# An attention and gMLP stack on one core: SyncE's queue in program order, later row sums, moved residual loads, a third buffer

## The chip, the cores and the metric

The kernel runs on one core of a Trainium2 chip. The metric is the device time of one execution in microseconds (us), the lower the better. Engines are written as in the profile: PE is the TensorE matmul, DVE the VectorE, ACT the ScalarE, POOL the GpSimd, and SP the SyncE, which here only issues DMA transfers.

## The reference, cut to what matters

```python
# x: 1 x 2048 x 512, bf16
def _A_ref(x, mem0, Wq, Wk, Wv, Wo, seg_len=32):     # attention with a memory of 8 rows
    mem = mem0
    for s in range(64):                              # one segment after the other
        h = concat([mem, x[:, 32*s:32*s+32]])        # 40 rows
        q, k, v = h @ Wq, h @ Wk, h @ Wv             # 32 heads of 128
        o = softmax(mask(q @ k.T * scale)) @ v       # per head
        o = o @ Wo
        mem = o[:, :8]                               # goes into the next segment
        outs.append(o[:, 8:])

def _B_ref(x, w_in, w_sp, b_sp, w_out):              # gMLP
    z = gelu(x @ w_in)                               # 2048 x 1376
    z1, z2 = z[..., :688], layernorm(z[..., 688:])
    g = w_sp @ z2 + b_sp[:, None]                    # over all 2048 rows
    return (z1 * g) @ w_out

for _ in range(2):                                   # same weights both times
    x = x + _A_ref(layernorm(x), ...)
    x = x + _B_ref(layernorm(x), ...)
```

The 64 segments of one attention block form a chain through `mem`. A gMLP has a stage of projections (16 row tiles of 128 rows, `x @ w_in`) and a stage of gates (16 tiles, `w_sp @ z2`, then `w_out`).

## The kernel before

PE, DVE and ACT keep the order in which the program was written (`ORDERED`). POOL and SP are ordered by the scheduler of the kernel's framework when the program is built. An engine's queue runs in its order.

```python
ORDERED = {PE, DVE, Activation}                                  # names shortened

# _consts: at the start
    nc.scalar.dma_start(bsp_bf[:], b_sp.rearrange("(t p) -> p t", p=P))
    nc.gpsimd.tensor_copy(bsp[:], bsp_bf[:])                     # POOL also issues the weight loads

# class _Rows: rows between attention and gMLP
    def apply(self, tb, MV, RS, first=False, x=None):            # normalise a row tile for attention
        # ... DVE writes xn
        nc.sync.dma_start(self.xn_d[...], xn[:])                 # store, then eight loads that wait for it
        # ... 4 x nc.sync.dma_start(preB[...], self.xn_d[...])
        # ... 4 x nc.sync.dma_start(pre, self.xn_d[...])

    def y_load(self, tb, first, eng, x=None, o=None):            # residual x and attention output o
        # ... eng.dma_start(x, ...), 4 x eng.dma_start(o <- oA_d), 4 x eng.dma_start(o <- oB_d)

    def y_add(self, tb, first, eng):
        o, x = self.y[tb]
        eng.tensor_tensor(out=..., in0=o, in1=x, op=ALU.add)     # the residual sum
        self.nc.sync.dma_start(self.xd[tb * P:(tb + 1) * P, :], o)

# b_block: the gMLP
        wsp_pool = ctx.enter_context(tc.tile_pool(name="b_wsp", bufs=2))
        ctx.enter_context(tc.manual_schedule(engines=ORDERED))

        def load_xnT(tt):                                        # transposed load, 3 buffers
            nc.sync.dma_start_transpose(out=xnT[tt][:], in_=rows.xb_d[...])
        def late_load(tb):                                       # the last four row tiles are summed here
            rows.y_load(tb, first, nc.gpsimd, x=..., o=o[:])
            rows.y_add(tb, first, nc.gpsimd)
        # late_norm(tb): DVE statistics and normalisation of two late tiles, SP stores them to xb_d

        for tt in range(3):
            load_xnT(tt)
        # ... w_out on POOL
        for tb in (NT - 4, NT - 3):
            late_load(tb)
        for tt in range(NT):
            project(tt)                                          # 12 matmuls into pz, two Gelu on ACT, DVE statistics
            if tt + 3 < NT:
                load_xnT(tt + 3)
            if tt in (3, 6):
                late_norm(NT - 4 + 2 * (tt // 6))
            if tt == 3:
                for tb in (NT - 2, NT - 1):
                    late_load(tb)
            if tt in (8, 11):
                load_wsp(tt // 11)
            if tt % 2 == 1:
                # ... DVE: RSz and NBz of two tiles
            elif tt > 1:
                normalise(tt - 2)                                # ACT: z2n
                normalise(tt - 1)
        # gates: gate(t), with product(t) behind it, which calls load_wsp(t + 2);
        # finish(t) writes rows t, and for t < 2 calls rows.apply(t, ...)

# a_block: after each segment s (tb, j4 = s // 4, s % 4)
            def spare():
                # ... if j4 == 3: rows.apply(tb + 2, ...)
            def tail():
                # ...
                if due:
                    ys.append(due.pop(0))
                    rows.y_load(ys[0], first, nc.sync)           # summed in the next segment
```

The softmax here doesn't subtract the row's maximum and nothing guards it: scores larger than these inputs give would overflow.

Of the kernel before, what the change touches and what calls it, by code (L numbers as in the profile page):

```python
# [14 lines left out]
P = 128  # L15
DM = 512
# [34 lines left out]
def _consts(ctx, tc, c, b_sp):  # L51
# [43 lines left out]
    c["maskM"] = maskM  # L95
    bsp_bf = tmp.tile([P, 16], BF16, name="bsp_bf")
    nc.scalar.dma_start(bsp_bf[:], b_sp.rearrange("(t p) -> p t", p=P))
    nc.gpsimd.tensor_copy(bsp[:], bsp_bf[:])
    c["bsp"] = bsp
    tctx.close()  # L100
    c.update(ident_bf=ident_bf, maskN=maskN, ones=ones, onesG=onesG)
# [37 lines left out]
class _Rows:  # L139
# [5 lines left out]

    def load(self, tb, first, eng):

        t = self.pool.tile([P, DM], BF16 if first else F32, name="ln_xb" if first else "ln_x")
        eng.dma_start(t[:], (self.x_in if first else self.xd)[tb * P:(tb + 1) * P, :])
        self.xs[tb] = t  # L150

    def apply(self, tb, MV, RS, first=False, x=None):
        nc = self.nc
        x = self.xs.pop(tb)[:] if x is None else x
        xn = self.pool.tile([P, DM], BF16, name="ln_xn", bufs=2)
        nc.vector.tensor_scalar(out=_perm(xn[:]) if first else xn[:], in0=_nat(x) if first else x, scalar1=MV[:, tb, 0:1],
                                scalar2=RS[:, tb:tb + 1], op0=ALU.subtract, op1=ALU.mult)
        nc.sync.dma_start(self.xn_d[M + tb * P:M + (tb + 1) * P, :], xn[:])
        preB = self.pool.tile([P, P], BF16, name="preB", bufs=2)
        for cg in range(4):  # L160
            nc.sync.dma_start(preB[32 * cg:32 * cg + 32, :],
                              self.xn_d[M + tb * P:M + (tb + 1) * P, 128 * cg:128 * cg + 128]
                              .rearrange("(j r) c -> j r c", j=4)[:, 24:32, :])
        self.preB[tb] = preB
        for j4 in range(4):
            t0 = tb * P + 32 * j4
            t = self.pool.tile([P, P], BF16, name="pre", bufs=9)
            nc.sync.dma_start(t[:], self.xn_d[t0:t0 + 32, :].rearrange("r (cg c) -> cg r c", cg=4))
            self.pre[4 * tb + j4] = t

    def y_load(self, tb, first, eng, x=None, o=None):
        if x is None:
            x = self.pool.tile([P, DM], BF16 if first else F32, name="y_xb" if first else "y_x")[:]
            o = self.pool.tile([P, DM], F32, name="y_o")[:]
        eng.dma_start(x, (self.x_in if first else self.xd)[tb * P:(tb + 1) * P, :])
        ot = o.rearrange("p (cg c) -> p cg c", cg=4)
        for j in range(4):
            eng.dma_start(ot[32 * j:32 * j + 24], self.oA_d[4 * tb + j + 1].rearrange("(cg r) c -> r cg c", cg=4)[8:32])
            r0 = 32 * (tb % 4) + 8 * j
            eng.dma_start(ot[32 * j + 24:32 * j + 32], self.oB_d[tb // 4, r0:r0 + 8, :].rearrange("r (cg c) -> r cg c", cg=4))  # L180
        self.y[tb] = (o, x)
# [18 lines left out]
def b_block(tc, c, rows, xd, MV_in, RS_in, MV_out, RS_out, w_in, w_sp, w_out, S, first, out_final=None):  # L200
# [4 lines left out]
    with ExitStack() as ctx:  # L205
        wp = ctx.enter_context(tc.tile_pool(name="b_w", bufs=1))
        mid = ctx.enter_context(tc.tile_pool(name="b_mid", bufs=1))
        gp = ctx.enter_context(tc.tile_pool(name="b_g", bufs=2))
        wsp_pool = ctx.enter_context(tc.tile_pool(name="b_wsp", bufs=2))
        zp = ctx.enter_context(tc.tile_pool(name="b_z", bufs=2))  # L210
        ps_pool = ctx.enter_context(tc.tile_pool(name="b_ps", bufs=1, space=PSUM))
        big = _Tagged(ps_pool, "big", 2)
        one = _Tagged(ps_pool, "one", 2)
        ctx.enter_context(tc.manual_schedule(engines=ORDERED))


        w_in_sb = wp.tile([P, KT, FF], BF16, name="w_in_sb")
# [17 lines left out]
            nc.sync.dma_start_transpose(out=xnT[tt][:], in_=rows.xb_d[tt * P:(tt + 1) * P, :].rearrange("t (kt s) -> t kt s", s=P))  # L235

        def late_load(tb):
            x = gp.tile([P, DM], F32, name="xs")[:]
            o = gp.tile([P, DM], F32, name="xo")
            rows.y_load(tb, first, nc.gpsimd, x=x[:, 0:DM // 2].bitcast(BF16) if first else x, o=o[:])  # L240
            rows.y_add(tb, first, nc.gpsimd)

        def late_norm(tb):
# [33 lines left out]
        for tt in range(NT):  # L277
            project(tt)
            if tt + 3 < NT:
                load_xnT(tt + 3)  # L280
            if tt in (3, 6):
                late_norm(NT - 4 + 2 * (tt // 6))
            if tt == 3:
                for tb in (NT - 2, NT - 1):
                    late_load(tb)
            if tt in (8, 11):
                load_wsp(tt // 11)
            if tt % 2 == 1:
                _rstd_dve(nc, zp, RSz[:, tt - 1:tt + 1], MVz[:, tt - 1:tt + 1, 1], 2)
                nc.vector.scalar_tensor_tensor(out=NBz[:, tt - 1:tt + 1], in0=MVz[:, tt - 1:tt + 1, 0], scalar=-1.0,  # L290
                                               in1=RSz[:, tt - 1:tt + 1], op0=ALU.mult, op1=ALU.mult)
            elif tt > 1:
                normalise(tt - 2)
                normalise(tt - 1)
# [15 lines left out]

        def product(t):
            del wsp[t]
            if t + 2 < NT:
                load_wsp(t + 2)
            u[t] = gp.tile([P, FH], BF16, name="u", bufs=1)
            nc.vector.scalar_tensor_tensor(out=u[t][:].rearrange("p (k f) -> p k f", k=2), in0=pg.pop(t)[:, 0:2, 0:344],
                                           scalar=c["bsp"][:, t:t + 1], in1=z1[:, t, :].rearrange("p (k f) -> p k f", k=2),
                                           op0=ALU.add, op1=ALU.mult)
            load_x(t)

        def turn_u(t):
# [1 line left out]
            for fc, (f0, fsz) in enumerate(FCH):  # L323
                nc.tensor.transpose(pT[0:fsz, fc * P:(fc + 1) * P], u[t][:, f0:f0 + fsz], ident_bf[:])
            del u[t]
            uT[t] = gp.tile([P, 6, P], BF16, name="uT")
            nc.scalar.copy(uT[t][:, 0:5, :].rearrange("p fc r -> p (fc r)"), pT[:, 0:640])
            nc.scalar.copy(uT[t][0:48, 5, :], pT[0:48, 640:768])

        def finish(t):  # L330
# [3 lines left out]
            del uT[t]  # L334
            xs = xt.pop(t)
            if out_final is not None:
                xob = gp.tile([P, DM], F32, name="xo")[:, 0:DM // 2].bitcast(BF16)
                nc.vector.tensor_tensor(out=_nat(xob), in0=_nat(py[:]), in1=_perm(xs[:]), op=ALU.add)
                nc.scalar.dma_start(out_final[t * P:(t + 1) * P, :], xob)
                return  # L340
            xo = gp.tile([P, DM], F32, name="xo")
            nc.vector.tensor_tensor(out=_perm(xo[:]), in0=_nat(py[:]), in1=_perm(xs[:]), op=ALU.add)
            nc.scalar.dma_start(xd[t * P:(t + 1) * P, :], xo[:])
            _stats(nc, zp, xo[:], MV_out[:, t, :])
# [18 lines left out]
def kernel(  # L363
# [34 lines left out]
    with tc.manual_schedule(engines=ORDERED):  # L398
        _ln_exp_table(nc)
        for tt in range(2):  # L400
            x = rp.tile([P, DM], BF16, name="x0", tag=("ln_xb", "y_xb")[tt])
            nc.sync.dma_start(x[:], x_in[tt * P:(tt + 1) * P, :])
            rows.xs[tt] = x
        m0 = rp.tile([M, DM], BF16, name="m0", tag="ln_xn", bufs=2)
        nc.sync.dma_start(m0[:], A_mem0.rearrange("b m d -> (b m) d"))
# [5 lines left out]
        _ln_consts(ctx, tc, c)  # L411
        MV, RS = c["MV"], c["RS"]
        for tt in range(2):
            _stats(nc, rp, rows.xs[tt][:], MV[0][:, tt, :])
            _rstd_act(nc, RS[0][:, tt:tt + 1], MV[0][:, tt, 1:2], c)
            rows.apply(tt, MV[0], RS[0], first=True)
        _consts(ctx, tc, c, B_b_sp)
# [30 lines left out]
def a_block(tc, c, rows, MV_in, RS_in, MV_out, RS_out, wqkv, Wo, S, first):  # L448
# [6 lines left out]
    with ExitStack() as ctx:  # L455
# [304 lines left out]
        for s in range(NSEG):  # L760
# [8 lines left out]
            def spare():  # L769
# [2 lines left out]
                if j4 == 0 and tb + 1 < NB:  # L772
                    ln_turn(tb + 1)
                if j4 == 2 and tb + 2 < NB and first:
                    _stats(nc, rows.pool, rows.xs[tb + 2][:], MV_in[:, tb + 2, :])
                    copies.append(lambda: _rstd_act(nc, RS_in[:, tb + 2:tb + 3], MV_in[:, tb + 2, 1:2], c))
                if j4 == 3 and tb + 2 < NB:
                    rows.apply(tb + 2, MV_in, RS_in, first=first)
# [1 line left out]
            def tail():  # L780
                if ys:
                    rows.y_norm(ys.pop(0), MV_out, RS_out)
                if tb % 4 == 3 and j4 == 0 and tb > 4:
                    due.extend(range(tb - 7, tb - 3))
                if due:
                    ys.append(due.pop(0))
                    rows.y_load(ys[0], first, nc.sync)

# [49 lines left out]
```

## Time and profile before

| | before |
|---|---|
| time, three first runs | 1990.4 to 1996.4 us, median 1995.61 |
| span of the profiled run, mean granted PE clock (1 is full speed) | 1993.9 us, 0.979 |
| PE, DVE, ACT, POOL busy | 90%, 63%, 53%, 7% |

A ledger of stages was made from marks in the timelines: the first and last masked copy (CAST_PREDICATED) that DVE makes in each attention block, the first `pz` matmul of PE and the last `NBz` of DVE in each gMLP. In us:

| stage | before |
|---|---|
| start, to the first masked copy | 62.0 |
| attention 1 | 743.1 |
| to the first `pz` | 27.7 |
| projections 1, to the last `NBz` | 69.5 |
| gates 1, to the first masked copy of attention 2 | 141.1 |
| attention 2 | 741.0 |
| to the first `pz` | 26.5 |
| projections 2 | 69.4 |
| gates 2, to the end | 113.7 |

Two groups of the page's costliest groups tell where PE waits. The columns are line, engine, operation, output and inputs, shapes and count; then busy time and mean ns; then the idle time ahead of the group and what ended most of it. Kernel before:

```profile
L489 PE MATMUL psm<-Wq_sb,hA 128*32 128x512 bf16 x4096 | 278.9, 388 | 28.7 <-DVE hA L598 27.7
L258 PE MATMUL pz<-w_in_sb,xnT 128*128 128x512 bf16 (+1 forms) x384 | 91.4, 405 | 44.6 <-ACT z L262 27.6
```

The first is the start of a segment in attention: 28.7 us of waits in 128 segments, nearly all for DVE's `hA`. The second is the projections of both gMLPs: 44.6 us of waits, mostly for ACT.

### The profile page before, as it was taken

The page shows a single profiled execution, that of the slowest core. Times are in us where ns is not written, and L with a number is a line of the kernel's source. Part 1 is how long each engine was busy: PE and PEld are TensorE (multiplying, and loading weights), DVE is VectorE, ACT ScalarE, POOL GpSimd, SP SyncE. Part 2 cuts the span into 40 slices and gives each one's busy share as a digit, 9 for nine tenths or more (in the row PEclk, how much of TensorE's full clock was granted, in tenths as well). Part 3 has the DMA queues.
Part 4 walks back from the last instruction along what each step waited for, and adds up shares of the span by engine and source line. Part 5 has one row for each costly group of instructions (what it writes and reads, how often), then busy time and mean ns, then how long its engine had stood idle before and what let it go on. Part 6 is the DMA issues. An engine that isn't in the chain of part 4 may idle for free.

```text
span 1993.9 us, 94918 instructions
## 1 busy us (share of the span) xinstructions
PE 1797.8 (90%) x43776; PEld 1035.5 (52%) x43776; DVE 1259.0 (63%) x2875; ACT 1047.9 (53%) x1880; POOL 138.0 (7%) x288
## 2 busy tenths in 40 slices
PE   2999999989998999777989999999899989996798
PEld 0555555545554555334545555555455555553355
DVE  1677677777777667572346667767767767774522
ACT  1566666656665666452136566666566656663411
POOL 5000000000000000230010000000000000005000
PEclk9999999999999999989999999999999999998899
DMA  8200000020012000625650000001200110017254
GB/s 306 69 21 20 18 19 17 24 79 17 18 30 73 18 15 29 152 72 123 148 155 24 20 20 22 21 20 50 69 21 21 60 58 22 15 53 187 55 139 111
DMA packets 179935, 120.08 MB, mean 60 GB/s; under 512 B 117280, under 2 KB 156976, under 8 KB 179536
## 3 DMA queue, kind: packets, MB, share of 16 engines
q1 hardware_dynamic: 158864, 70.43, 13.9%
q0 software_dynamic: 9376, 28.88, 4.4%
q10 hardware_dynamic: 11296, 14.70, 2.4%
q8 instruction: 342, 5.60, 1.2%
q14 instruction: 57, 0.47, 0.1%
HBM read 59.29 MB, written 33.69 MB: 47 GB/s over the span
## 4 chain that ended last, share of the span: by engine, by line
PE 37%; DVE 7%; ACT 5%; DMA 3%; issue 2%; SPq 1%; POOL 1%; POOLq 0%; DVEq 0%; ACTq 0%
PE psm L489 12%; PE pg L308 6%; PE pw L546 5%; PE psb L489 4%; DVE KA L626 2%; PE py L333 2%; ACT rows L622 2%; ACT E L650 2%; PE psO L669 2%; PE psS L646 1%; PE pwB L555 1%; DMA wspT<-in_B_w_sp_dram 1%; DVE E L653 1%; PE psM L713 1%; PE psD L722 1%
## 5 line engine op out<-in xcount | busy, mean ns | idle before, releaser
L489 PEld LDWEIGHTS <-hA 128*32 128x32 bf16 x12288 | 311.3, 97 | 329.1 <-DVE hA L598 64.3
L622 ACT CAST rows<-psm 128x512 bf16<-128x512 f32 x512 | 299.8, 586 | 197.9 <-PE psm L489 197.9
L489 PE MATMUL psm<-Wq_sb,hA 128*32 128x512 bf16 x4096 | 278.9, 388 | 28.7 <-DVE hA L598 27.7
L546 PE MATMUL pw<-Wo_sb,uT 128*32 128x128 bf16 x16640 | 267.4, 220 | 28.8 <-issue 20.2
L546 PEld LDWEIGHTS <-uT 128*32 128x32 bf16 x16640 | 245.2, 97 | 69.5 <-issue 30.8
L489 PE MATMUL psm<-Wk_sb,hA 128*32 128x512 bf16 x4096 | 273.7, 385 | 0.0
L489 PE MATMUL psv<-Wv_sb,hA 128*32 128x512 bf16 x4096 | 268.0, 382 | 0.0
L626 DVE STREAM_TRANSPOSE QQ<-rows 128x512 bf16<-128x512 bf16 x256 | 182.0, 711 | 95.6 <-ACT rows L622 94.5
L685 DVE TENSOR_TENSOR uT<-psO,Rt 128x384 bf16<-128x384 f32 x256 | 138.1, 539 | 126.5 <-ACT Rt L675 126.5
L626 DVE STREAM_TRANSPOSE KA<-rows 128x512 bf16<-128x512 bf16 x256 | 182.0, 711 | 42.8 <-ACT rows L622 41.0
L650 ACT ACTIVATE E<-psS 128x448 bf16<-128x448 f32 x256 | 140.0, 547 | 107.6 <-PE psS L646 107.6
L308 PE MATMUL pg<-z2n,wspT 128*128 128x344 bf16 x1024 | 166.1, 316 | 14.9 <-ACT z2n L269 7.6
L632 DVE CAST VA<-psv 128x512 bf16<-128x512 f32 x256 | 175.7, 686 | 2.3
L591 POOL COPY QQ<-QTB 128x256 bf16<-128x256 bf16 x128 | 51.2, 401 | 1431.3 <-PE psS L646 870.1
L646 PEld LDWEIGHTS <-KA 128*64 128x64 bf16 x2048 | 79.8, 113 | 127.8 <-DVE KA L626 126.5
L675 ACT ACTIVATE Rt<-Rt 128x1024 f32<-128x1024 f32 x128 | 135.4, 1058 | 4.1
L308 PEld LDWEIGHTS <-wspT 128*128 128x128 bf16 x1024 | 96.5, 99 | 71.5 <-issue 15.5
L258 PE MATMUL pz<-w_in_sb,xnT 128*128 128x512 bf16 (+1 forms) x384 | 91.4, 405 | 44.6 <-ACT z L262 27.6
L489 PEld LDWEIGHTS <-hB 128*32 128x32 bf16 x3072 | 75.9, 97 | 106.4 <-issue 38.4
L674 ACT ACTIVATE Rt<-psD 128x1024 f32<-128x1024 f32 x128 | 128.6, 1005 | 0.0
L730 DVE TENSOR_TENSOR uT<-psO,Rm 128x128 bf16<-128x128 f32 x256 | 62.8, 286 | 93.3 <-PE psO L669 93.1
L646 PE MATMUL psS<-QQ,KA 128*64 128x80 bf16 x2048 | 109.9, 208 | 10.1
(113 smaller groups left out, 2265.1 us busy)
## 6 DMA issues: line engine op xcount, KB each, us to landing
oA_d<-o_sb SPq DMA_DIRECT2D x130, 64.0 KB
Wo_sb<-in_A_Wo_dram POOLq DMA_DIRECT2D x8, 1024.0 KB, 13.5
xs<-xd ACTq DMA_DIRECT2D x32, 256.0 KB
xd<-y_o SPq DMA_DIRECT2D x24, 256.0 KB
y_o<-oA_d SPq DMA_DIRECT2D x96, 48.0 KB
Wq_sb<-in_A_Wq_dram POOLq DMA_DIRECT2D x8, 512.0 KB, 7.4
Wk_sb<-in_A_Wk_dram POOLq DMA_DIRECT2D x8, 512.0 KB, 11.1
xn_d<-ln_xn SPq DMA_DIRECT2D x32, 128.0 KB
```

The source lines that it names most:

```text
L258: nc.tensor.matmul(pz[:, c0:c1], lhsT=xnT[tt][:, kt, :], rhs=w_in_sb[:, kt, c0:c1], start=(kt == 0), stop=(kt == KT - 1))
L308: nc.tensor.matmul(pg[t][:, k, 0:344], lhsT=wsp[t][:, st, :], rhs=z2n[:, st, 344 * k:344 * k + 344], start=(st == 0), stop=(st == NT - 1))
L489: nc.tensor.matmul(ps[32 * cg:32 * cg + 32, :], lhsT=lhs(kt, cg), rhs=rhs(kt, cg), start=(kt == 0), stop=(kt == KT - 1), tile_position=(0, ...
L546: nc.tensor.matmul(po[32 * cg:32 * cg + 32, 0:128], lhsT=lhs[:, n, :], rhs=wo_rhs(h, cg), start=(h == 0), stop=(h == H - 1), tile_position ...
L622: nc.scalar.copy(r[:], ps[:])
L626: nc.vector.transpose(out=QQ[:, j % 2, :, 0:32] if j < 2 else KA[:, j % 2], in_=r[:])
L632: nc.vector.tensor_copy(VA[:, r].rearrange("p i e -> p (i e)"), ps)
L646: nc.tensor.matmul(pS[64 * g:64 * g + 64, i, c0:80 if K is KA else 112], lhsT=K[:, r, n:n + 2, :].rearrange("p h k -> p (h k)"), rhs=q if ...
L650: nc.scalar.activation(out=E[:, r], in_=pS, func=ACT.Exp, scale=scale)
L674: nc.scalar.activation(out=o, in_=in_, func=ACT.Ln)
L675: nc.scalar.activation(out=o, in_=o, func=ACT.Exp, scale=-1.0)
L685: nc.vector.tensor_tensor(out=hview(uT_nxt, 2 * r, 2 * r + 2, 8, 32), in0=oview(2 * r, 2 * r + 2, 8, 32), in1=Rr[:, :, :, 0:24], op=ALU.mult)
```

## The change

The diff has four intents. The cast of `bsp` leaves POOL, whose queue the first weights stand in. A residual load of a segment is no longer written where the next block's rows are (j4 = 3). The `wspT` tiles of the gates get a third buffer. In the gMLP SP joins the engines in program order, and the last four row tiles are normalised later (after tiles 5 and 9 instead of 3 and 6). To make room in memory, some row tiles share buffers.

```diff
-    nc.gpsimd.tensor_copy(bsp[:], bsp_bf[:])
+    nc.vector.tensor_copy(bsp[:], bsp_bf[:])
... (bf16 row tiles become views of float32 tiles: load, y_load)
-        wsp_pool = ctx.enter_context(tc.tile_pool(name="b_wsp", bufs=2))
+        wsp_pool = ctx.enter_context(tc.tile_pool(name="b_wsp", bufs=3))
-        ctx.enter_context(tc.manual_schedule(engines=ORDERED))
+        ctx.enter_context(tc.manual_schedule(engines=ORDERED | {mybir.EngineType.SP}))
         def late_load(tb):
-            x = gp.tile([P, DM], F32, name="xs")[:]
-            o = gp.tile([P, DM], F32, name="xo")
-            rows.y_load(tb, first, nc.gpsimd, x=x[:, 0:DM // 2].bitcast(BF16) if first else x, o=o[:])
+            x, o = None, None
+            if tb % 2:
+                x = gp.tile([P, DM], F32, name="xs")[:]
+                o = gp.tile([P, DM], F32, name="xo", bufs=1)[:]
+            rows.y_load(tb, first, nc.gpsimd, x=x, o=o)
             rows.y_add(tb, first, nc.gpsimd)
-            if tt in (3, 6):
-                late_norm(NT - 4 + 2 * (tt // 6))
-            if tt == 3:
+            if tt in (5, 9):
+                late_norm(NT - 4 + 2 * (tt // 9))
+            if tt == 5:
                 for tb in (NT - 2, NT - 1):
                     late_load(tb)
-            if tt in (8, 11):
-                load_wsp(tt // 11)
+            if tt in (9, 11, 13):
+                load_wsp((tt - 9) // 2)
-            if t + 2 < NT:
-                load_wsp(t + 2)
+            if t + 3 < NT:
+                load_wsp(t + 3)
... (uT and xo with one buffer)
-                if due:
+                if due and (j4 != 3 or tb + 2 >= NB):
```

More of the change, by code (lines that the diff above doesn't have):

```diff
@@ L146, in load @@
     def load(self, tb, first, eng):
-        t = self.pool.tile([P, DM], BF16 if first else F32, name="ln_xb" if first else "ln_x")
-        eng.dma_start(t[:], (self.x_in if first else self.xd)[tb * P:(tb + 1) * P, :])
+        t = self.pool.tile([P, DM], F32, name="ln_x")[:]
+        t = t[:, 0:DM // 2].bitcast(BF16) if first else t
+        eng.dma_start(t, (self.x_in if first else self.xd)[tb * P:(tb + 1) * P, :])
         self.xs[tb] = t
@@ L153, in apply @@
         nc = self.nc
-        x = self.xs.pop(tb)[:] if x is None else x
+        x = self.xs.pop(tb) if x is None else x
         xn = self.pool.tile([P, DM], BF16, name="ln_xn", bufs=2)
@@ L172, in y_load @@
         if x is None:
-            x = self.pool.tile([P, DM], BF16 if first else F32, name="y_xb" if first else "y_x")[:]
+            x = self.pool.tile([P, DM], F32, name="y_x")[:]
             o = self.pool.tile([P, DM], F32, name="y_o")[:]
+        x = x[:, 0:DM // 2].bitcast(BF16) if first else x
         eng.dma_start(x, (self.x_in if first else self.xd)[tb * P:(tb + 1) * P, :])
@@ L325, in turn_u @@
             del u[t]
-            uT[t] = gp.tile([P, 6, P], BF16, name="uT")
+            uT[t] = gp.tile([P, 6, P], BF16, name="uT", bufs=1)
             nc.scalar.copy(uT[t][:, 0:5, :].rearrange("p fc r -> p (fc r)"), pT[:, 0:640])
@@ L336, in finish @@
             if out_final is not None:
-                xob = gp.tile([P, DM], F32, name="xo")[:, 0:DM // 2].bitcast(BF16)
+                xob = gp.tile([P, DM], F32, name="xo", bufs=1)[:, 0:DM // 2].bitcast(BF16)
                 nc.vector.tensor_tensor(out=_nat(xob), in0=_nat(py[:]), in1=_perm(xs[:]), op=ALU.add)
@@ L340, in finish @@
                 return
-            xo = gp.tile([P, DM], F32, name="xo")
+            xo = gp.tile([P, DM], F32, name="xo", bufs=1)
             nc.vector.tensor_tensor(out=_perm(xo[:]), in0=_nat(py[:]), in1=_perm(xs[:]), op=ALU.add)
@@ L400 @@
         for tt in range(2):
-            x = rp.tile([P, DM], BF16, name="x0", tag=("ln_xb", "y_xb")[tt])
-            nc.sync.dma_start(x[:], x_in[tt * P:(tt + 1) * P, :])
+            x = rp.tile([P, DM], F32, name="x0", tag=("ln_x", "y_x")[tt])[:, 0:DM // 2].bitcast(BF16)
+            nc.sync.dma_start(x, x_in[tt * P:(tt + 1) * P, :])
             rows.xs[tt] = x
@@ L413 @@
         for tt in range(2):
-            _stats(nc, rp, rows.xs[tt][:], MV[0][:, tt, :])
+            _stats(nc, rp, rows.xs[tt], MV[0][:, tt, :])
             _rstd_act(nc, RS[0][:, tt:tt + 1], MV[0][:, tt, 1:2], c)
@@ L774, in spare @@
                 if j4 == 2 and tb + 2 < NB and first:
-                    _stats(nc, rows.pool, rows.xs[tb + 2][:], MV_in[:, tb + 2, :])
+                    _stats(nc, rows.pool, rows.xs[tb + 2], MV_in[:, tb + 2, :])
                     copies.append(lambda: _rstd_act(nc, RS_in[:, tb + 2:tb + 3], MV_in[:, tb + 2, 1:2], c))
```

## The prediction

> **What bounds the kernel now.** I read the page first, then each stage by its own timelines and waits.
>
> ```profile
> span 1993.9 us, 94918 instructions
> PE 1797.8 (90%) x43776; PEld 1035.5 (52%) x43776; DVE 1259.0 (63%) x2875; ACT 1047.9 (53%) x1880; POOL 138.0 (7%) x288
> ...
> PE   2999999989998999777989999999899989996798
> ...
> DMA  8200000020012000625650000001200110017254
> ```
>
> PE is the bound, at 90%. A slice of the 40 is 49.8 us. PE is short in the first slice (start), in slices 17 to 19 and 37 to 38 (the two gMLPs, 820 to 1022 us and 1806 to 1994), and by a tenth in a few slices of the attention blocks. Elsewhere PE is full and this change leaves PE's own work alone: in the comparison of the two programs' orders PE's list is the same, 87,554 rows. So only PE's holes can change. There are four kinds, one for each part of the change.
>
> **Start.** The timeline of POOL:
>
> ```profile
> 12.54 0.41 POOL L79 TENSOR_SCALAR_AFFINE_SELECT maskf<-maskf 32x32 f32<-32x32 f32 x2
> 19.63 0.20 POOL L98 CAST bsp<-bsp_bf 128x16 f32<-128x16 bf16 x1 [6.68 <-DMA bsp_bf<-in_B_b_sp_dram]
> 20.09 0.56 POOL L442 DMA_DIRECT2D Wq_sb<-in_A_Wq_dram  x1 [0.27 <-issue]
> ```
>
> POOL sits 6.68 us before a tiny cast, and the other 16 weight loads stand behind it. The windows table has 383 to 390 GB/s from 8 to 16 us, 82 GB/s from 16 to 20, near 400 from 28 on; PE then follows the weights until its first segment at 49.17.
>
> **Attention.** DVE writes one CAST_PREDICATED (L597) per 32-row segment. The distance between two of them is a segment: about 11.8 us, about 12.5 with a residual sum. Four pairs stand out: 15.93 and 14.63 (from 426.7), 15.66 and 13.02 (from 623.1), 15.38 and 13.50 (from 1408.3), 17.34 and 12.94 (from 1601.9). Timelines of SP and DVE in the third:
>
> ```profile
> 1412.41 2.18 SPq L168 DMA_DIRECT2D pre<-xn_d  x4
> 1414.71 0.41 SPq L603 DMA_DIRECT2D oA_d<-o_sb  x1
> 1415.22 0.38 SPq L197 DMA_DIRECT2D xb_d<-ln_xn  x1
> 1415.65 0.40 SPq L178 DMA_DIRECT2D y_o<-oA_d  x1
> ...
> 1421.31 0.69 DVE L185 TENSOR_TENSOR y_o<-y_o,y_x 128x512 f32<-128x512 f32 x1 [3.84 <-DMA y_o<-oB_d]
> ```
>
> The fourth residual load of a group stands on SP behind the next block's rows (`preB`, `pre`). It starts at 1415.65 instead of about 1411.5, DVE waits 3.84 us in order, and hA, then PE, wait behind it. PE's next 64 matmuls take 5.35 us instead of 3.55, at a lower clock.
>
> **gMLP, projections.** PE's timeline, first gMLP:
>
> ```profile
> 832.78 9.77 PE L258 MATMUL pz<-w_in_sb,xnT 128*128 128x512 bf16 x36 [5.58 <-issue]
> 845.76 10.75 PE L258 MATMUL pz<-w_in_sb,xnT 128*128 128x512 bf16 x48 [3.21 <-DMA xnT<-xb_d]
> 862.48 6.26 PE L258 MATMUL pz<-w_in_sb,xnT 128*128 128x512 bf16 x24 [5.97 <-ACT z L262]
> 881.00 11.88 PE L258 MATMUL pz<-w_in_sb,xnT 128*128 128x512 bf16 x48 [6.45 <-ACT z L262]
> ```
>
> PE isn't the limit here. From 884 to 902 NBz comes every 6.15 us for a pair of tiles, a loop through ACT (z, z2n) and DVE (statistics, 13 small operations). The late rows add 5.3 us of DVE work per pair of rows (two such pairs), and the second one waits some 1.5 us for POOL. The 3.21 us is tile 3's transposed load, behind two `wspT` transposes.
>
> **gMLP, gates.** The same timeline later has four holes in the first gMLP:
>
> ```profile
> 928.81 1.92 PE L308 MATMUL pg<-z2n,wspT 128*128 128x344 bf16 x12 [1.09 <-DMA wspT<-in_B_w_sp_dram]
> 940.52 3.60 PE L308 MATMUL pg<-z2n,wspT 128*128 128x344 bf16 x12 [4.80 <-DMA wspT<-in_B_w_sp_dram]
> 956.20 1.92 PE L308 MATMUL pg<-z2n,wspT 128*128 128x344 bf16 x12 [0.39 <-DMA wspT<-in_B_w_sp_dram]
> 977.42 1.92 PE L308 MATMUL pg<-z2n,wspT 128*128 128x344 bf16 x12 [0.88 <-DMA wspT<-in_B_w_sp_dram]
> ```
>
> The second gMLP has none: a gate there takes 6.73 us throughout.
>
> **What the Trainium skill says.** "DMA: Bandwidth & Descriptors", section "Anatomy of one DMA — SWDGE (gpsimd) path": DMA engines do not wait on semaphores; the wait happens on the issuing sequencer before dispatch. The trace agrees: SP's store of the first late sum is issued at 845.44, right after POOL ends it at 845.41, and nothing else passes on SP in between. So a store that waits holds up every load written behind it; my main point rests on this. The same section gives a fixed cost of about 2 us for such a load; here the chain has 2.42 us for `xo<-oB_d`. "TensorE: Matmul & The Clock Gate", Part 1: PE's clock is halved after idleness and comes back after some microseconds of work; the trace agrees (granted clock 0.50 at 832 to 836 and at 880 to 884, after the holes).
>
> **The change part by part.**
>
> 1. *The cast of `bsp` to DVE.* POOL ends its masks at about 13, so the weights start some 7 us earlier. They bound the start until 49.17; small row loads compete with them. **-6 us**. DVE's cast stands after memsets that end at 27.6, when `bsp_bf` has landed: nothing.
> 2. *Residual loads not at j4 = 3.* In the order the fourth sum moves one segment on, while its loads keep their place on SP, so they have a segment more. A pair becomes 11.8 + 12.5 = 24.3 us. (30.56 - 24.3) + (28.68 - 24.3) + (28.88 - 24.3) + (30.28 - 24.3) = **-21 us**.
> 3. *Third `wspT` buffer.* `wspT` for gate t+3 is issued after gate t, so 13 us remain for loads that the chain shows at 5 to 7.5 us. Removed: 1.09 + 4.80 + 0.39 + 0.88 = 7.2, and about 1 us of lower clock. **-8 us**, first gMLP only. One `xo` and one `uT` less cost nothing: their last use lies a gate back.
> 4. *SP in program order, sums later.* In the changed order SP has: three `xnT`, **both stores of the first late sums**, six `xnT`, two `xb_d`, **both stores of the second sums**, then `xnT` for tile 9. Before, a scheduler had put `xnT` loads ahead of those stores.
>    - Tile 3: in the same POOL order of size (1.45 us for `w_out` from 834.6, some 14 issues at 0.57 us, a wait for `w_out`, two sums) I get the second sum's end at about 849 to 851 (851.4 before). Then store and issue 1.5 us and about 2.8 us to land: tile 3 at about 853.5 instead of 845.8. Loss 7.7 us, but this gap no longer has a late norm after it.
>    - With statistics of tile 3 at 857.9: NBz(2,3) at 862 (859.3 before); (4,5) with the first late norm, 862 + 6.15 + 5.3 = 873.5; (6,7) at 879.6 (877.9 before).
>    - Tile 9: the second sums take 13.1 us from the end of the first late norm, as before (857.0 to 870.1), so 871.1 + 13.1 = 884.2, and `xnT` is there at about 888. The loop wants it at about 878.5: 9.5 us more. Before, tile 9 didn't stand behind a sum.
>    - NBz(8,9) = 879.6 + 6.15 + 9.5 + 5.3 = 900.6, three more pairs: 919, against 902.4. Rounded **+17 us**. The second gMLP has the same order and the same 57 us from tile 3 to the last NBz: **+17 us**.
>    - `wspT` out of the way of tile 3 gives 3.2 us, already in these times.
>
> Sum: -6 - 21 - 8 + 34 = -1 us, so 1994.6. The four gains rest on measured waits; the loss on a modelled queue. I shade it by 4 us because the sums may come sooner with their own tiles and without `wspT` traffic: **1991 us**.
>
> **Rivals.**
> - *The stores cost little.* If POOL's sums end by about 843 and the second by 878, tiles 3 and 9 are in time; the late norm no longer waits, and each projection stage is 3 to 5 us shorter: about 1953. For: the purpose of the change, and separate `y_x`/`y_o`. Against: the issues alone, 16 at 0.57 us after `oB_d` lands at 833, need until 842 plus landing and two sums of 1.2 us.
> - *A wait comes back in attention.* The moved sum meets b_units and a fuller DVE at j4 = 1: half of part 2 lost, about 2001. Against: DVE is at 63%, and other segments with a sum take 12.5.
> - *The start gives nothing*, if `preB` lands later by as much: 1997.
> - *Gates stay bound by `wspT` throughput*, not by latency: +8. Against: the second gMLP sustains one per 6.73 us.
>
> **Range and chances.** The loss has the largest doubt, 34 with perhaps 15 either way; attention 21 with 5; start and gates 14 with 5. Together about 17: 1969 to 2008. Over 2% faster means below 1955.7; that needs the first rival whole: 0.05. Over 2% slower, above 2035.5, needs another stall of 40 us: 0.02.
>
> **What would show it.** First segment of PE at about 43 instead of 49. No DVE wait for `y_o` at the four pairs, and pairs of about 24.3. No `wspT` among PE's waits. In each gMLP two new holes of 8 to 11 us before PE's tiles 3 and 9, put down to `xnT`, with SP's next transposes right after the stores of late sums; the stage from first pz to last z2n near 80 to 88 us instead of 71. Were those holes missing, or the stage shorter than before, step 4 is wrong.

## More of the kernel before

The kernel before differed a little from chip to chip (medians 1995.99 to 2001.72), so kernels are compared by ratios against the kernel before on the same chip.

## The result, and the profile after

Ratios here and below are the mean time of one kernel's runs over the mean of the other's runs of the same rounds, so they are not quite the ratio of the medians quoted.

The changed kernel took 1994.43 us (median of 4 runs, 1992.86 to 1995.65), the kernel before 1995.99 us (median of 4, 1990.4 to 1996.4). The ratio is 0.9998, with a 95% interval from 0.9979 to 1.0018: the same time. The page of the kernel after:

```profile
span 1992.1 us, 94947 instructions
...
PE   3899999999999999657989999999999999985798
...
L494 PE MATMUL psm<-Wq_sb,hA 128*32 128x512 bf16 x4096 | 273.5, 383 | 13.8 <-DVE hA L603 12.8
L263 PE MATMUL pz<-w_in_sb,xnT 128*128 128x512 bf16 (+1 forms) x384 | 92.6, 409 | 74.2 <-DMA xnT<-xb_d 53.5
```

Against the row of before, PE's row of slices has gained in the attention blocks (slices 9, 13, 29 and 33 went from 8 to 9 tenths) and lost in the projections: slices 17 and 18 went from 7 and 7 to 6 and 5, slices 36 and 37 from 9 and 6 to 8 and 5. The waits at the start of a segment fell from 28.7 to 13.8 us. Those of the projections rose from 44.6 to 74.2 us and changed their name: 53.5 us of them are now for the transposed loads `xnT`. The ledger (us):

| stage | before | after | difference | predicted |
|---|---|---|---|---|
| start | 62.0 | 56.4 | -5.6 | -6 |
| attention 1 and 2 | 743.1 + 741.0 | 731.9 + 726.8 | -25.4 | -21 |
| projections 1 and 2 | 69.5 + 69.4 | 84.3 + 86.1 | +31.5 | +34 |
| gates 1 | 141.1 | 140.7 | -0.4 | -8 |
| to the first `pz`, twice | 27.7 + 26.5 | 26.3 + 28.4 | +0.5 | 0 |
| gates 2 | 113.7 | 111.3 | -2.4 | 0 |
| span | 1993.9 | 1992.1 | -1.8 | -1 |

**Start.** POOL's timeline after (start, duration, engine, line, operation, output and inputs):

```profile
12.51 0.41 POOL L79 TENSOR_SCALAR_AFFINE_SELECT maskf<-maskf 32x32 f32<-32x32 f32 x2
12.87 0.56 POOL L447 DMA_DIRECT2D Wq_sb<-in_A_Wq_dram  x1
```

The weight load now follows the masks with no gap; its place was 20.09 before. PE's first segment starts at 41.67 instead of 49.17, and the first masked copy is 5.6 us earlier.

**Attention.** The third of the four pairs of segments, SP's timeline and then DVE's:

```profile
1408.99 2.18 SPq L169 DMA_DIRECT2D pre<-xn_d  x4
1411.28 0.41 SPq L608 DMA_DIRECT2D oA_d<-o_sb  x1
1411.79 0.37 SPq L199 DMA_DIRECT2D xb_d<-ln_xn  x1
1412.22 0.40 SPq L180 DMA_DIRECT2D y_o<-oA_d  x1
```

```profile
1415.12 0.29 DVE L602 CAST_PREDICATED pre<-maskM,pw 128x128 bf16<-128x128 uint16 x1
1424.37 0.69 DVE L187 TENSOR_TENSOR y_o<-y_o,y_x 128x512 f32<-128x512 f32 x1
```

SP issues the residual loads still behind the rows of the next block (`pre`), but DVE makes the sum only at 1424.37, one segment later, and its line has no wait in brackets, where before it had 3.84 us. The four pairs are 23.89, 23.37, 23.96 and 23.23 us, after 30.56, 28.68, 28.88 and 30.28.

**Projections.** PE's timeline in the first gMLP after, then SP's in the same stretch, then the two POOL sums that end last in their pairs:

```profile
814.57 8.81 PE L263 MATMUL pz<-w_in_sb,xnT 128*128 128x512 bf16 x36 [3.88 <-issue]
832.67 11.18 PE L263 MATMUL pz<-w_in_sb,xnT 128*128 128x512 bf16 x48 [9.28 <-DMA xnT<-xb_d]
844.47 4.81 PE L263 MATMUL pz<-w_in_sb,xnT 128*128 128x512 bf16 x24 [0.62 <-ACT z L267]
866.34 11.41 PE L263 MATMUL pz<-w_in_sb,xnT 128*128 128x512 bf16 x48 [17.06 <-DMA xnT<-xb_d]
883.83 8.87 PE L263 MATMUL pz<-w_in_sb,xnT 128*128 128x512 bf16 x36 [6.08 <-ACT z L267]
```

```profile
829.51 0.32 SPq L188 DMA_DIRECT2D xd<-xo  x1
829.94 12.81 SPq L237 DMA_TRANSPOSE xnT<-xb_d  x6
849.96 0.82 SPq L199 DMA_DIRECT2D xb_d<-ln_xn  x2
857.76 0.33 SPq L188 DMA_DIRECT2D xd<-y_o  x1
863.33 0.33 SPq L188 DMA_DIRECT2D xd<-xo  x1
863.75 8.25 SPq L237 DMA_TRANSPOSE xnT<-xb_d  x4
```

```profile
828.33 1.15 POOL L187 TENSOR_TENSOR xo<-xo,xs 128x512 f32<-128x512 f32 x1 [0.35 <-DMA xo<-oB_d]
862.15 1.15 POOL L187 TENSOR_TENSOR xo<-xo,xs 128x512 f32<-128x512 f32 x1 [1.65 <-DMA xo<-oA_d]
```

After three tiles (36 matmuls) PE has a hole of 9.28 us, and after nine tiles (36 + 48 + 24 matmuls) one of 17.06 us, both put down to `xnT`. SP tells why: the next transposes are issued at 829.94 and 863.75, each 0.1 us after a store of a late sum (829.51 + 0.32, 863.33 + 0.33). Each of these stores starts 0.03 us after POOL ends its sum (828.33 + 1.15 = 829.48, 862.15 + 1.15 = 863.30). PE had been done with the three tiles that filled the buffers since 823.38 (814.57 + 8.81) and 849.28 (844.47 + 4.81). In the kernel before, the scheduler had put three transposes ahead of the first store and three more ahead of the second:

```profile
840.68 3.81 SPq L235 DMA_TRANSPOSE xnT<-xb_d  x3
845.44 0.33 SPq L186 DMA_DIRECT2D xd<-xo  x1
849.57 5.84 SPq L235 DMA_TRANSPOSE xnT<-xb_d  x3
855.76 1.02 SPq L186 DMA_DIRECT2D xd<-xo  x1
```

The second gMLP has the same two holes, 9.98 and 17.18 us. The windows of these stretches (busy time and count of PE, PEld, DVE, ACT, POOL; granted clock; DMA share; GB/s) show that no engine had over 0.2 us more work. Before:

```profile
832.80:902.30 69.50, 50.01 (x220) 23.36 (x221) 44.89 (x188) 33.65 (x46) 23.36 (x37) 0.84 0.42 97
```

After:

```profile
814.60:898.90 84.30, 49.14 (x220) 23.11 (x221) 45.07 (x188) 33.83 (x46) 22.90 (x36) 0.78 0.35 87
```

**Gates.** One of four holes stayed. PE's and SP's timelines after:

```profile
925.75 1.92 PE L313 MATMUL pg<-z2n,wspT 128*128 128x344 bf16 x12 [0.70 <-DMA wspT<-in_B_w_sp_dram]
936.85 3.62 PE L313 MATMUL pg<-z2n,wspT 128*128 128x344 bf16 x12 [4.20 <-DMA wspT<-in_B_w_sp_dram]
```

```profile
922.20 0.52 SPq L159 DMA_DIRECT2D xn_d<-ln_xn  x1
925.93 2.63 SPq L162 DMA_DIRECT2D preB<-xn_d  x4
928.60 2.19 SPq L169 DMA_DIRECT2D pre<-xn_d  x4
930.89 6.76 SPq L257 DMA_TRANSPOSE wspT<-in_B_w_sp_dram  x2
```

PE waits until 936.85 for a `wspT` that SP issues at 930.89, behind the nine transfers of row tile 1. From 922.72 to 925.93 SP issues nothing, between the store to `xn_d` and the first load that reads what it wrote. I had not foreseen this.

### The profile page after: what moved, and what is told of

Same layout as the page of the kernel before. It is cut to its first block, busy times and chain, and to the rows that moved or that the text cites. A ratio compares the mean times of both kernels' runs of the same rounds, so it can differ in the third digit from the quotient of the medians.

```text
span 1992.1 us, 94947 instructions
## 1 busy us (share of the span) xinstructions
PE 1787.7 (90%) x43776; PEld 1033.7 (52%) x43776; DVE 1259.4 (63%) x2876; ACT 1050.9 (53%) x1880; POOL 138.2 (7%) x287
## 3 DMA queue, kind: packets, MB, share of 16 engines
q0 software_dynamic: 9376, 28.88, 4.2%
## 4 chain that ended last, share of the span: by engine, by line
PE 39%; DVE 7%; ACT 5%; issue 2%; DMA 2%; POOL 1%; SPq 0%; DVEq 0%; POOLq 0%; ACTq 0%
PE psm L494 12%; PE pg L313 7%; PE pw L551 5%; PE psb L494 4%; DVE KA L631 2%; PE py L338 2%; ACT rows L627 2%; PE psO L674 2%; ACT E L655 2%; PE pwB L560 2%; PE psS L651 1%; DVE E L658 1%; PE psM L718 1%; PE psD L727 1%; PE pT L329 1%
## 5 line engine op out<-in xcount | busy, mean ns | idle before, releaser
L494 PE MATMUL psm<-Wq_sb,hA 128*32 128x512 bf16 x4096 | 273.5, 383 | 13.8 <-DVE hA L603 12.8
L551 PEld LDWEIGHTS <-uT 128*32 128x32 bf16 x16640 | 244.4, 97 | 67.6 <-issue 29.6
L263 PE MATMUL pz<-w_in_sb,xnT 128*128 128x512 bf16 (+1 forms) x384 | 92.6, 409 | 74.2 <-DMA xnT<-xb_d 53.5
L494 PEld LDWEIGHTS <-hB 128*32 128x32 bf16 x3072 | 76.5, 97 | 101.0 <-issue 32.5
```

Source lines behind the costliest of these rows:

```text
L263: nc.tensor.matmul(pz[:, c0:c1], lhsT=xnT[tt][:, kt, :], rhs=w_in_sb[:, kt, c0:c1], start=(kt == 0), stop=(kt == KT - 1))
L494: nc.tensor.matmul(ps[32 * cg:32 * cg + 32, :], lhsT=lhs(kt, cg), rhs=rhs(kt, cg), start=(kt == 0), stop=(kt == KT - 1), tile_position=(0, ...
L551: nc.tensor.matmul(po[32 * cg:32 * cg + 32, 0:128], lhsT=lhs[:, n, :], rhs=wo_rhs(h, cg), start=(h == 0), stop=(h == H - 1), tile_position ...
```

## The experiments

Theory: the parts act in their stages and add up; the loss comes from the stores of the late sums in SP's program order, and at the gates the same program order takes the third buffer's gain back. Rivals: the loss comes from the later place of the late norms, from POOL's work, or from the shared buffers; the gate holes come from `wspT` throughput; the equal times come about by chance on one chip. All ten kernels below gave correct results. e1 to e4 ran on one chip, e5 to e8 on a second, e9 and e10 on a third, each with the kernel before beside them.

### e1_bsp_only: the kernel before with the cast moved

```diff
-    nc.gpsimd.tensor_copy(bsp[:], bsp_bf[:])
+    nc.vector.tensor_copy(bsp[:], bsp_bf[:])
```

> The kernel before with only the bsp cast moved from POOL to VectorE. Theory: POOL no longer sits 6.7 us before the weight loads, so the first CAST_PREDICATED of the trace comes at about 56.4 us as in the changed kernel (62.0 before) and nothing else moves: 5 to 6 us off, about 1990. Rival (the early gain is lost again later, in a stage that follows a clock of its own): 1995 to 1996.

Measured: 1993.19 us (median of 6), before 2001.72 (median of 11); ratio 0.9966 (0.9947 to 0.9986), which is about 6.8 us. The start took 56.2 us, so the rival in which `preB` lands later by as much falls. That the gain isn't lost again later rests on the ratio alone, whose interval allows 3 to 11 us. The profiled run, the second slowest of the six, had a span of 1995.0 us, no shorter than before: its attention 1 took 745.3 us and its first gates 145.1, 2.2 and 4.0 us more than in the kernel before, the latter with 9.1 us of waits for `wspT` instead of 7.2.

### e2_j4_only: the kernel before with the residual rule

```diff
-                if due:
+                if due and (j4 != 3 or tb + 2 >= NB):
```

> The kernel before with only the rule that the fourth residual load waits for the next segment. Theory: the four pairs of long segments (about 30.6, 28.7, 28.9 and 30.3 us) become about 24 us each, VectorE waits no more for y_o there, and nothing else moves: 21 to 26 us off, about 1972. Rival (part of the gain of the attention stages in the changed kernel comes from the other parts, through transfers or buffers): 10 us or less off, 1985 or more.

Measured: 1975.88 us (4 runs), ratio 0.9881 (0.986 to 0.9902), about 24 us. Its attention stages took 730.8 and 726.8 us, the pairs 23.21 to 23.82. This one line gives all that the changed kernel gains in the attention stages (26.5 us against 25.4); the rival in which a wait comes back in attention falls.

### e3_store_pool: the changed kernel, late sums stored by POOL

POOL makes these sums, so in POOL's own order the store stands right behind its sum.

```diff
-    def y_add(self, tb, first, eng):
+    def y_add(self, tb, first, eng, store=None):
-        self.nc.sync.dma_start(self.xd[tb * P:(tb + 1) * P, :], o)
+        (store or self.nc.sync).dma_start(self.xd[tb * P:(tb + 1) * P, :], o)
-            rows.y_add(tb, first, nc.gpsimd)
+            rows.y_add(tb, first, nc.gpsimd, store=nc.gpsimd)
```

> The changed kernel with the stores of the eight late sums issued by POOL, which makes the sums, instead of SyncE. Theory (SyncE held by those stores makes the holes before tiles 3 and 9): the four holes of 9 to 17 us go, a projection stage falls from 84 to 86 us to 66 to 69, the kernel to about 1960 (1955 to 1966). Rival (the tiles are late because the sums themselves and POOL's loads are late, or because the transposed loads are slow in themselves): the holes stay, 1990 or more.

Measured: 1961.44 us (4 runs), ratio 0.9807 (0.9789 to 0.9825). The projections took 67.2 and 68.7 us. SP's and PE's timelines of e3:

```profile
816.28 20.00 SPq L237 DMA_TRANSPOSE xnT<-xb_d  x7
```

```profile
817.59 8.76 PE L263 MATMUL pz<-w_in_sb,xnT 128*128 128x512 bf16 x36 [8.29 <-issue]
827.03 4.82 PE L263 MATMUL pz<-w_in_sb,xnT 128*128 128x512 bf16 x24 [0.68 <-DMA xnT<-xb_d]
```

Seven transposes run through without a break, and PE's hole before tile 3 is 0.68 us. One wait for `xnT` is left, 7.78 us before the last three tiles of the second gMLP, where e5 has 6.93 us for ACT. Nothing in the program but the issuing engine of eight stores differs (four in each gMLP). POOL's queue, which the scheduler orders, ends the first pair's sums even later, 17.2 us after the first `pz` instead of 14.9, so earlier sums aren't the reason. The same sums, buffers and late norms are there, so the rivals of POOL's work, of the shared buffers and of the norms' place can't explain the loss. The stages give 84.3 + 86.1 - 67.2 - 68.7 = 34.5 us back. The spans differ by 32.5 us (1992.1 and 1959.6), the ratios, which come from two chips and have intervals of some 4 us to each side, by 0.0191 or about 38 us.

### e4_sp_sched: the changed kernel, SP left to the scheduler

```diff
-        ctx.enter_context(tc.manual_schedule(engines=ORDERED | {mybir.EngineType.SP}))
+        ctx.enter_context(tc.manual_schedule(engines=ORDERED))
```

> The changed kernel with SyncE left to the scheduler in the gMLP again; all else as changed. Theory: the scheduler puts transposed loads ahead of the stores, so the holes of 9 to 17 us go, but two or three wspT loads stand before tile 3 again (a hole of 3 to 6 us): projection stages of 68 to 73 us, about 1966 (1960 to 1974). Rival (later sums and the shared buffers cost the time, not SyncE's order): 1988 or more.

Measured: 1963.38 us (4 runs), ratio 0.9819 (0.9798 to 0.984). The projections took 71.9 and 68.9 us, and the first gates 132.3 us instead of 140.7. At tile 3 PE waits 5.88 and 3.55 us for `xnT` behind `wspT` loads, as expected, and it has no wait for `wspT` at the gates. SP's timeline of e4 there:

```profile
889.28 8.86 SPq L257 DMA_TRANSPOSE wspT<-in_B_w_sp_dram  x2
898.19 0.57 SPq L159 DMA_DIRECT2D xn_d<-ln_xn  x1
```

The scheduler puts one more `wspT` load ahead of the first row tile than program order does. So one line of the change, the order of SP, cost 84.3 + 86.1 - 71.9 - 68.9 = 29.6 us in the projections and 8.4 us at the gates, 38 in all (some 36 by the ratios, over two chips).

### e5_rows_later: e3, with the row tiles' transfers behind a `wspT` load

The diff is cut: `apply` hands back its nine transfers, and the gates write them later.

```diff
 def apply(...):                       # the nine transfers become apply_io
+        if later:
+            return lambda: self.apply_io(tb, xn)
 # product(t), after load_wsp(t + 3):
+            if rows_io:
+                rows_io.pop()()
 # finish(t):
-                rows.apply(t, MV_out, RS_out, x=xo[:])
+                rows_io.append(rows.apply(t, MV_out, RS_out, x=xo[:], later=True))
```

> The kernel with POOL's stores (1961 us), and in the first gMLP the transfers of the next block's first two row tiles are written behind the next wspT load instead of ahead of it; SyncE stays in program order, three wspT buffers. Theory (in program order those nine transfers per tile, which wait for xn_d to land, hold the wspT loads of gates 4 and 5): PE waits for wspT no more in the first gMLP (5.3 us there), the time from the last NBz to the next attention block falls from 140.4 to about 132 us as with the scheduler, the kernel to about 1953. Rival (the transposed loads of w_sp are slow there for transfers beside them): the waits stay or move by a gate, 1960 to 1962.

Measured: 1955.39 us (4 runs), ratio 0.9787 (0.9764 to 0.981). The first gates took 134.3 us, and no wait of PE for `wspT` is left, with SP still in program order. This shows that the hole of 4.20 us at the gates stood on the row tiles' transfers ahead of the load, not on the throughput of `wspT` loads.

### e6_second_pair: the changed kernel, only the last two stores on POOL

```diff
-            rows.y_add(tb, first, nc.gpsimd)
+            rows.y_add(tb, first, nc.gpsimd, store=nc.gpsimd if tb >= NT - 2 else None)
```

> The changed kernel with only the second pair's stores (the last two row tiles) issued by POOL. Theory: the hole before tile 9 (17.1 and 17.2 us in the changed kernel) goes, down to 6 or 7 us of waiting for ACT, the hole before tile 3 (9.3 and 10.0) stays; by the prediction's terms 7.7 us of each stage belong to tile 3 and 9.5 to tile 9, so projection stages of about 75 us and 1975 us. Rival (the two holes are one: what the first costs is made up at the second): stages of 67 to 70 us, 1962, or of 84, 1994.

Measured: 1976.3 us (4 runs), ratio 0.989 (0.9865 to 0.9915). The projections took 74.5 and 75.3 us. PE's timeline of e6:

```profile
829.84 11.32 PE L263 MATMUL pz<-w_in_sb,xnT 128*128 128x512 bf16 x48 [8.77 <-DMA xnT<-xb_d]
841.78 4.81 PE L263 MATMUL pz<-w_in_sb,xnT 128*128 128x512 bf16 x24 [0.62 <-ACT z L267]
853.17 11.79 PE L263 MATMUL pz<-w_in_sb,xnT 128*128 128x512 bf16 x48 [6.58 <-ACT z L267]
```

The hole at tile 3 stays; at tile 9 the 17 us for `xnT` have become 6.58 us for ACT, the loop's own pace. The two holes are separate and can be sized: tile 9's pair of stores costs 84.3 - 74.5 = 9.8 and 86.1 - 75.3 = 10.8 us a stage, tile 3's 74.5 - 67.2 = 7.3 and 75.3 - 68.7 = 6.6 us, each from single profiled runs. A hole of 17 us thus costs 10, because some 6.6 us of it would have been waited for ACT in any case.

### e7_sched_two_wsp: e4 with two `wspT` buffers

```diff
-        wsp_pool = ctx.enter_context(tc.tile_pool(name="b_wsp", bufs=3))
+        wsp_pool = ctx.enter_context(tc.tile_pool(name="b_wsp", bufs=2))
-            if tt in (9, 11, 13):
+            if tt in (9, 11):
                 load_wsp((tt - 9) // 2)
-            if t + 3 < NT:
-                load_wsp(t + 3)
+            if t + 2 < NT:
+                load_wsp(t + 2)
```

> The changed kernel with SyncE left to the scheduler in the gMLP and two wspT buffers instead of three. Theory (the third buffer does take away the wspT waits, and only SyncE's program order gave that back): waits for wspT come back in the first gMLP as in the kernel before (7 us of holes, last NBz to the next block about 141 us against 132.3), about 1971 to 1973. Rival (the gain at the gates is the schedule's or the DMA traffic's, not the buffer's): about 132 us there, 1963.

Measured: 1972.38 us (5 runs), ratio 0.9871 (0.9846 to 0.9897). The first gates took 142.5 us against 132.3 in e4. PE's waits of e7 (total, times, longest) have:

```profile
PE pg L313 <- DMA wspT<-in_B_w_sp_dram: 6.1, 4, 4.3
```

The third buffer is worth about 10 us where the order of SP lets it work, a little more than predicted (the ratios of e4 and e7, from two chips, differ by 0.0052, also about 10 us). The size of part 3 was right; it did not come about in the changed kernel.

### e8_sums_early: e3 with the late norms at their old places

```diff
-            if tt in (5, 9):
-                late_norm(NT - 4 + 2 * (tt // 9))
-            if tt == 5:
+            if tt in (3, 6):
+                late_norm(NT - 4 + 2 * (tt // 6))
+            if tt == 3:
```

> The kernel with POOL's stores (1961 us), and the late sums' norms at tiles 3 and 6 as in the kernel before instead of 5 and 9. Theory (the later place of the norms is worth the DVE's waits for POOL's sums, some 2 to 4 us a stage): projection stages of 69 to 72 us instead of 67 to 69, 1965 to 1969. Rival (VectorE's own 5.3 us per norm is all that counts, wherever it stands): 1961.

Measured: 1961.29 us (4 runs), ratio 0.982 (0.9795 to 0.9846), projections 67.3 and 68.1 us, as in e3. I had expected a loss of 2 to 4 us a stage. DVE's timeline of e8 has the wait for POOL's sum that I counted on:

```profile
853.94 0.69 DVE L135 BATCH_NORM_STATS2 bnst<-xo 128x6 f32<-128x512 f32 x1 [2.33 <-POOL xo L187]
```

It cost nothing on the path: the stage is as long without it. The ratios of e3 and e8, from two chips, differ by 0.0013, less than their intervals. With POOL's stores the later norms of the change are thus worth nothing that shows; with SP's stores this was not tried.

### e9_norm_one_later: e5 with ACT's normalisation one projection later

The remaining waits of the projections are for ACT, which normalises the last pair ahead of the next tile's Gelu. This version lets a Gelu go first.

```diff
             if tt % 2 == 1:
                 ...                                              # RSz, NBz of the pair
-            elif tt > 1:
-                normalise(tt - 2)
-                normalise(tt - 1)
+                if tt > 1:
+                    normalise(tt - 3)
+                    normalise(tt - 2)
```

> The kernel of the row loads behind wspT (1955 us), with the ScalarE normalisation of a pair of tiles written one projection later, so that ScalarE meets NBz when VectorE has it. Theory (the projection stage is a loop of 6.1 us a pair through ScalarE and VectorE in which VectorE idles 1.4 us): the loop falls to VectorE's own work, 4.7 to 5.3 us a pair, and a stage of 64 to 68 us loses 5 to 8 us; the last normalisations may give 1 us back: 1940 to 1946. Rival (the loop is bound by VectorE's small operations or by PE at a lower clock): 1953 to 1956.

Measured: 1947.38 us (median of 5), before 1999.78 (median of 11); ratio 0.974 (0.9716 to 0.9764), faster than both kernels. The projections took 62.7 and 63.2 us, 1.6 and 4.3 us less than in e5, where I had expected 5 to 8 a stage; the total ratio fell by 0.0047, some 9 us, a comparison over two chips. The loop itself did fall as expected: late in the stage `NBz` comes every 4.6 to 4.7 us for a pair, where e5 has 6.12. But PE still stands before its last three tiles, now for `xnT`, in the first and the second gMLP:

```profile
866.58 8.66 PE L269 MATMUL pz<-w_in_sb,xnT 128*128 128x512 bf16 x36 [7.55 <-DMA xnT<-xb_d]
1820.66 9.47 PE L269 MATMUL pz<-w_in_sb,xnT 128*128 128x512 bf16 x36 [8.65 <-DMA xnT<-xb_d]
```

In e5 PE waited 7.00 and 6.93 us there for ACT. SP issues these transposes (863.66 and 1818.02) behind the stores of the second pair's normalised rows (860.64 and 1814.55) and one `wspT` load, in program order: again an entry that waits. No run removes this one, so that it is the next limit is read from the timelines and not shown.

### e10_after_again: the changed kernel, unaltered, on another chip

> The changed kernel itself, unaltered, beside the kernel before on another chip, to have its ratio next to those of the experiments. If its gains and losses cancel whatever the chip, the ratio lies within 0.995 to 1.003; if the result of the first comparison was that chip's, it lies below 0.99.

Measured: 2000.04 us (6 runs), before 1999.78 (11 runs); ratio 1.0 (0.9981 to 1.0019). Projections took 85.5 and 84.9 us, attention 732.5 and 729.0. The cancelling is not an accident of one chip.

The ledgers side by side, in us. No edit of e5 touches the projections, yet they differ from e3's by 2.9 and 1.2 us, so differences of that size between two profiled runs prove nothing:

| stage | before | after | e3 | e4 | e5 | e9 |
|---|---|---|---|---|---|---|
| attention 1 | 743.1 | 731.9 | 730.1 | 731.0 | 732.7 | 734.5 |
| projections 1 | 69.5 | 84.3 | 67.2 | 71.9 | 64.3 | 62.7 |
| gates 1 | 141.1 | 140.7 | 140.4 | 132.3 | 134.3 | 134.2 |
| attention 2 | 741.0 | 726.8 | 726.2 | 727.9 | 727.4 | 728.9 |
| projections 2 | 69.4 | 86.1 | 68.7 | 68.9 | 67.5 | 63.2 |
| span | 1993.9 | 1992.1 | 1959.6 | 1958.2 | 1952.0 | 1945.7 |

## Why the prediction was right, point by point

The time was predicted at 1991.0 us and measured at 1994.43, within 2% and well inside the range. The sum of the steps, 1994.6, was nearer than the shaded number, so the shading of 4 us had no ground. The stated range isn't the stated doubt either: 17 us to each side of 1991 give 1974 to 2008, and nothing in the working leads to the lower end of 1969.

1. **The start, right.** Predicted -6, measured -5.6 in the ledger and about -6.8 in e1 alone. The cast on DVE cost nothing that shows.
2. **The residual loads, right, a little under-sized.** Predicted pairs of 24.3 us; measured 23.2 to 24.0. Predicted -21, measured -25.4 in the attention stages (24.0 of it in the four pairs) and about -24 in e2.
3. **The third buffer, wrong in this kernel.** Predicted -8 and no `wspT` among PE's waits; the first gates fell by only 0.4 us, and a wait of 4.20 us stayed. The failed step is "so 13 us remain for loads that the chain shows at 5 to 7.5 us". It took the moment at which a load is allowed for the moment at which it is issued. The load itself had the predicted size: issued at 930.89, it let PE go on at 936.85, 6.0 us later. But gate 2, behind which it is written, was over by 918.92 (DVE then works on its product), so 12.0 of the 13 us had passed when SP issued it. I applied program order on SP to the late sums in step 4, but not to the two row tiles in the gates, whose transfers wait there for `xn_d`. e4 and e5 remove these from in front of the load and bring 132.3 and 134.3 us; e7 shows that the buffer itself is worth what was predicted, or a little more. The rival "gates stay bound by `wspT` throughput" had about the right number, +8, with a cause that e4 and e5 exclude.
4. **SP in program order, right in mechanism and in size.** Predicted +17 a stage, measured +14.8 and +16.7. Both holes are where they were predicted, with SP's transposes right behind the stores. The second is longer than the 8 to 11 us named as a sign, 17.06 and 17.18 us: the sign left out the loop's own wait for ACT (6.58 us in e6), which the term of 9.5 us had rightly counted apart. Counted from the first `pz`, the model had the second sum at 16 to 18 us, tile 3's data at 20.7 and tile 9's at 55; measured were 14.9 (829.48 - 814.57), 18.1 and 51.8. The second pair's sums were put at 13.1 us and took 863.30 - 850.23 = 13.1. The two terms, 7.7 and 9.5 us, came out at about 7 and 10 in e6. e3 and e4 confirm the cause from two sides.

That the sum lies within 0.2 us of the measured time is luck: 7.6 us too much gain at the gates stood against 4.4 too little in attention, 2.5 too much loss in the projections, and some 2 us of small differences at the edges of stages that I do not explain. What isn't luck are the large terms, predicted at -35 and +34 us and measured at -31 and +31, which the runs show one by one. Of the rivals, "the stores cost little" put 1953 us on a kernel without the loss; e3 reaches 1961 with the stores out of SP's way, and 1955 once the gates are mended too (e5).

The statement of the Trainium skill that the main point rests on, that a transfer's wait lies on the issuing sequencer, is borne out by e3: with the stores of the same sums on another sequencer, SP's transposes run through and the holes of 9 and 17 us are gone. The one on the clock, that PE's drops after idleness, agrees with the windows: the granted clock in the first projections fell from 0.84 to 0.78 as the holes grew.

## What to carry to other kernels

Putting SP's queue in program order made each store that waits a barrier for the loads written after it, here with holes of 9 and 17 us. Issue such a store from the engine that makes its data, or write it behind the loads that are needed soon, and check every waiting entry of that queue, in every stage, not only those the change is about. When a change of several parts moves the time by nothing, make a ledger by stage before calling the parts useless: here one line was worth 24 us and another cost 38, and the version that keeps the first, works around the second and adds one change of order on ACT is 2.6% faster than the kernel before.

## What the Trainium skill lacked or had wrong

- "DMA: Bandwidth & Descriptors", section "Issuing engines are not separate DMA queues", says that issuing from several engines saves only the sequencer's time to initiate a transfer, "which is usually small relative to the DMA itself". It leaves out the waiting on the sequencer, of which the same page tells elsewhere: moving eight stores from SyncE to GpSimd took the span from 1992.1 to 1959.6 us (ratio to the kernel before 0.9807, against 0.9998), with the same bytes. The table "Rules for kernel authors" of that page has the same gap.
- The same page's section "Anatomy of one DMA — SWDGE (gpsimd) path" says where the wait is, and leaves it to the reader what follows for the transfers behind it. Here a store that waited for POOL's sum held back the transposes of three buffers that were free, and PE stood for 9.28 and 17.06 us.
- The same section's table gives about 50 ns for dispatch and, for the descriptor work, no figure but "small, variable". On GpSimd in this kernel the trace has 0.50 to 0.67 us of its queue for the issue of one load of `oA_d` or `oB_d`, and the loads and sums of two row tiles took 13.1 us.
- The section "DMA Transpose (X-bar)" of that page has no time for which a transposed load occupies the queue that issues it, and the page's cycle counts for such an instruction are for small tiles or for copies within the on-chip memory. Here one of `xnT` (128 x 512, bf16), issued alone, took about 1.2 us of SyncE's queue, and one of `wspT` (128 x 2048, bf16) mostly 1.8 to 2.7 us.
